# Tail values stored in tile order, block 14's own rows, one output round moved and the first feed-forward sums moved

## The chip, the cores and the metric

The program runs on one core of a Trainium2 chip. The core's engines run side by side, each with its own instruction queue: TensorE (PE; its weight loads are listed as PEld), VectorE (DVE), ScalarE (ACT), GpSimd (POOL) and SyncE (SP), which here only issues DMA transfers. They meet at semaphores: an instruction, or a separate semaphore instruction ahead of it, waits until a count is reached. The metric is the device time of one execution in microseconds, as the median of the runs. Smaller is better.

## The reference

The input x has 2048 rows of 640. A recurrent attention with 32 heads of 128 runs over 64 segments of 32 rows, carrying 8 memory rows from each segment to the next; a feed-forward part with a squared ReLU follows.

```python
for s in range(n_seg):                          # 64 segments
    xs = x[:, s * seg_len:(s + 1) * seg_len, :] # x is layernormed
    h = jnp.concatenate([mem, xs], axis=1)      # 8 + 32 rows
    q, k, v = (einsum('btd,dhe->bhte', h, W) for W in (Wq, Wk, Wv))
    scores = einsum('bhqe,bhke->bhqk', q, k) * scale
    scores = where(mask, scores, -1e9)          # memory columns open, the rest causal
    p = softmax(scores)
    o = einsum('bhte,hed->btd', einsum('bhqk,bhke->bhqe', p, v), Wo)
    mem = o[:, :M, :]                           # the next segment needs these rows
    outs.append(o[:, M:, :])
h  = x + concat(outs)
h2 = h + (relu(layernorm(h) @ w1 + b1) ** 2) @ w2 + b2
```

Only the 8 memory rows make the loop sequential. Segment s+1 can start once the memory rows of o are there; the other rows of a segment's output can be finished later.

## The kernel before

**Tiling.** A block is 128 rows, so four segments; there are 16 blocks (`NB`) and 64 steps (`NS`), one `step(b, sp)` for each segment. A step's projections take 32 rows: the 8 memory rows that the step before made and the first 24 rows of the segment (`HD`). The last 8 rows of a segment, its tail (`TL`), do not depend on the memory in q, k and v, so the tails of a block's four segments are projected together, 32 rows at a time, ahead of time. The weights wq, wk, wv and wo lie in SBUF, loaded once by SP at the start (`load_w`, `load_wo`).

**A step.** `step` writes the order of the work out by hand, and every engine executes it in that order: query and key projections (L234 in the helper `proj`), ScalarE's copies to `row` tiles and VectorE's 32 by 32 transposes to qT and kT; scores of the memory rows for each half of the heads (`scores`, L497); their softmax (`soft1`, `soft2`, `soft3`), which gives the transposed probabilities pB; value projections; token scores; the values of the memory rows for each half (`values`, L543 and L548, the second for the tail values `vt4`), copied to `oT` by ScalarE (`values_out`, L246); the output projection `wo_rounds` into the PSUM tile pw in 16 rounds of four matmuls (L270); `wo_out`, which adds the parts (L285 to L287) and transposes the new memory rows to `hT` (L382), with which the next step's query projection begins. Rounds 0 to 7 need the first half of the heads in `oT`, rounds 8 to 15 the second half. In a common step rounds 0 to 3 stand before `values` of the second half, and rounds 4 to 15 behind it. The token values of the segment before (`token_values`, L423 and L428) end the step on TensorE.

**Filler work.** TensorE is given independent work in between, from the list `fill`: the tail projections of coming blocks in units of five per half (`tail_units`), and the output projection of whole blocks' tails in ten units per block (`wo_tail_units`), which read the tail's attention output in `oTts` (two buffers for even and odd blocks). The plan has for each group of units a step by which it is due and a step from which it may be done. `portion(s)` takes units in the order of the due steps: as many as keep the running total at `round(8.15 * s)`, at most nine, and more where a due step has come. Other short work waits in lists too: `late` (at the start of a step, by a budget), `mid` (after the memory rows are made, two entries a step) and `nook` (one entry a step, between VectorE's token score subtraction, L657, and its sum, L664, while ScalarE computes the exponentials).

**Tail values.** `tail_out` writes the value rows of a block's tails from a `row` tile (or, at the start, from tiles that stand empty, `parked`) to the DRAM tile `vt_d`, and `tails_v_in` reads them back in the order that `values` needs, `vt4`. Before, `vt_d` has the layout of block, quarter of the columns (4), row (128), 256 columns. A write is one transfer of 128 rows by 2 pieces (L345); a read is four transfers of 32 partitions each (L402), one for each group of heads, and it fills vt4 a block ahead, in the second step of the block before. At the start the values of blocks 0 to 9 are projected; block 0's are written and read by POOL's queue (its last three quarters are read by SP), the others by SP, behind the load of wo.

**The end.** The step before last and the last fill in the first feed-forward tile's preparation: `prep_load`, `prep_sum0` (adding the attention output and x, L778), `prep_stats0`, `prep_norm0` and a transposing DMA, each for four blocks of rows in steps 57 to 63. In the last step SP loads w1 into the space of wq, after the query projections, and then the feed-forward part runs over four tiles of 512 rows (L994 and L1046).

Of the kernel before, what the change touches and what calls it, by code (L numbers as in the profile page):

```python
# [12 lines left out]
BF16 = mybir.dt.bfloat16  # L13
# [3 lines left out]
def kernel(  # L17
# [16 lines left out]
    nc = tc.nc  # L34
    _, S, D = A_x.shape
# [302 lines left out]
    def tail_out(b, which, n, ps, dve=False):  # L338
        row, wait = parked.pop(0) if which == "v" and 0 < b and parked else (rowtile()[:], False)
        evac_row(which, row, ps, dve)  # L340
        if which == "v":
            eng = nc.sync if b else nc.gpsimd

            def write():
                eng.dma_start(out=vt_d[b, 2 * n:2 * n + 2].rearrange("j r f -> r j f"),  # L345
                              in_=row.rearrange("r (j f) -> r j f", j=2))
            if wait:
                writes.append(write)
            else:
                write()  # L350
            return
        if n == 0:
            tails.setdefault(b, {})[which] = s2.tile([128, H, 32], BF16, tag=which + "Tt", name=which + "Tt")
        dst = tails[b][which]
        late.append((0.71, lambda: flip(row, dst, n), 4 * b - (which == "k")))

    def wo_tail_out(b, ps):
        o = wo_out(ps)
# [4 lines left out]
    def wo_tail_units(b):  # L363
        st = {}

        def out():
            wo_tail_out(b, st["ps"])

        def unit(k):
            def f():  # L370
                if k == 0:
                    st["ps"] = mmtile()
                wo_rounds(lambda p: oTts[b % 2][:, p, :], st["ps"], range(k * 16 // 10, (k + 1) * 16 // 10))
                return (False, out) if k == 9 else None
            return f
        return [unit(k) for k in range(10)]
# [13 lines left out]
        q = tails[b]["q"][:].rearrange("p h (k s) -> p h s k", s=4)[:, n * 16:(n + 1) * 16, sp, :]  # L390
        nc.gpsimd.tensor_copy(out=qT[:, n * 16:(n + 1) * 16, 0:TL], in_=q)

    vt4s = {}
    vt_d = dram.tile([NB, 4, 128, 2 * E], BF16)

    def tails_v_in(b, eng, s0=0, s1=4):

        if s0 == 0:
            vt4s[b] = s2.tile([128, 4, 2, E], BF16, tag="vt4", name="vt4")
        src = vt_d[b].rearrange("j (g k s) f -> g j k (s f)", g=G, s=4)  # L400
        for g in range(G):
            eng.dma_start(out=vt4s[b][32 * g:32 * g + 32, s0:s1].rearrange("p s u e -> p (s u e)"),  # L402
                          in_=src[g][:, :, s0 * 2 * E:s1 * 2 * E])

    def store_main(o, s):
        for q in range(4):
# [24 lines left out]
    def token_out(s, po):  # L431
        for h in range(2):
            gs = slice(2 * h, 2 * h + 2)
            nc.scalar.copy(out=oTg[:, gs, :, :, 0:SEG],  # L434
                           in_=po[1][h][:, :, 0:256].rearrange("p g (n j q) -> p g n j q", n=2, q=32))
        nc.gpsimd.tensor_copy(out=oTts[s // 4 % 2][:, :, s % 4 * TL:(s % 4 + 1) * TL], in_=oT[:, :, 0:TL])

    def spread(n):
        for a0, a1, f in ((0, 120, 3), (120, 128, 1)):
# [14 lines left out]
    def step(b, sp, v=None):  # L454
# [172 lines left out]
        skv = view()  # L627
        po = po_tiles()
        if last:
            run(fill, max(1, (len(fill) - 3) // 2), held, True)  # L630
            token_values(s - 1, *prevs[-2], po)
            token_out(s - 1, po)
            settle(held, True)
            run(fill, 2, held)
            settle(held, True)
            causal(skv)
        else:
            ahead = 0 if ready else (len(fill) + 1) // 2
            left = len(fill) - ahead
            run(fill, (ahead - 1) // 2, held, True)  # L640
            values(0, pT0, po[1][0])
            values_out(0, po[1][0])
            if not ready:
                nc.scalar.copy(out=v[:, 768:1024], in_=ps1[:, 256:512])
            run(fill, len(fill) - left, held)
            pw = chn.tile([128, 512], F32, tag="ch", name="pw")
            if not ready:
                wo_rounds(lambda p: oT[:, p, M:NK], pw, range(4))
            values(1, pT1, po[1][1])
            causal(skv)  # L650
            values_out(1, po[1][1])
            settle(held, True)
# [23 lines left out]
        if not last:  # L676
# [2 lines left out]
                    run(fill, SEG0[k])  # L679
                    wo_rounds(lambda p: oT[:, p, M:NK], pw, [2 * k + h for h in (0, 1, 8, 9)])  # L680
            else:
                wo_rounds(lambda p: oT[:, p, M:NK], pw, range(4, 16))
            o = wo_out(pw, ((s + 1) // 4, (s + 1) % 4), weigh)
            if s > 1:
                store_main(o, s - 2)
# [109 lines left out]
    def prep_sum0(k):  # L795
        pre[k] = prep_sum(0, k, pre[k])
# [100 lines left out]
            plan += [(4 * b - 3 + (which == "k"), 4 * b - 5, u[DC * n:DC * n + DC]) for n in range(2)]  # L897
    for b in range(10, NB):
        u = tail_units(b, "v")
        plan += [(b - 8 if b < 12 else 20 + 4 * (2 * b - 24 + n), 1 if b < 12 else 7, u[DC * n:DC * n + DC]) for n in range(2)]  # L900
    for b in range(NB - 1):
        plan.append((min(4 * b + 8, NS - 2), 4 * b + 5, wo_tail_units(b)))
    plan.sort(key=lambda p: p[0])
    begun, paced = [], [0]

    def portion(s):
        n = round(8.15 * s) - paced[0]
        got = []
        while True:
            if not begun:  # L910
# [14 lines left out]
    for b in range(NB):  # L925
        for sp in range(4):
# [25 lines left out]
            e = b * 4 + sp - (NS - 7)  # L952
            if (b, sp) == (1, 0):
                ffn_biases()
            if (b, sp) == (2, 0):
                nc.gpsimd.tensor_copy(out=b1f[:], in_=b1b[:])
            if 0 <= e < NK4:
                pre[e] = prep_load(0, e)
            if 1 <= e <= NK4:
                mid.append(lambda e=e: prep_sum0(e - 1))  # L960
            if 2 <= e <= NK4 + 1:
                late.insert(0, (1.15, lambda e=e: prep_stats0(e - 2), b * 4 + sp))
                mid.append(lambda e=e: prep_norm0(e - 2))
# [125 lines left out]
```

## Time and profile before

| what | value |
|---|---|
| median of 3 runs | 952.71 us (950.44 to 955.07) |
| profiled execution | 951.48 us, its span 949.7 us |
| granted TensorE clock, mean | 0.996 |
| busy share: PE, DVE, ACT, POOL | 97%, 72%, 60%, 33% |
| first query matmul of step 1 | 62.89 us |
| first query matmul of step 63 | 807.61 us |
| first feed-forward matmul | 818.33 us |
| SP's transfers: o_all stores, vt reads, vt writes | 320, 64, 30 |

The span goes from the first to the last instruction of the program; the profiled execution's time has some 1.8 us around it. The start up to 62 us is the loading of the weights; then come 62 steps of about 12 us; from 818 us on the feed-forward. An engine's busy share is an average over these stages. A matmul's record lasts longer than the distance between matmuls' starts, since they are pipelined and four run beside each other on 32 columns of the array each, so distances between starts are what counts for TensorE. In the timeline a row merges equal instructions that follow each other: start, time, engine, line, operation, operands, count, and in brackets the engine's idle time before it with what ended it.

### The profile page before, as it was taken

The page shows a single profiled execution, that of the slowest core. Times are in us where ns is not written, and L with a number is a line of the kernel's source. Part 1 is how long each engine was busy: PE and PEld are TensorE (multiplying, and loading weights), DVE is VectorE, ACT ScalarE, POOL GpSimd, SP SyncE. Part 2 cuts the span into 40 slices and gives each one's busy share as a digit, 9 for nine tenths or more (in the row PEclk, how much of TensorE's full clock was granted, in tenths as well). Part 3 has the DMA queues.
Part 4 walks back from the last instruction along what each step waited for, and adds up shares of the span by engine and source line. Part 5 has one row for each costly group of instructions (what it writes and reads, how often), then busy time and mean ns, then how long its engine had stood idle before and what let it go on. Part 6 is the DMA issues. An engine that isn't in the chain of part 4 may idle for free.

```text
span 949.7 us, 56126 instructions
## 1 busy us (share of the span) xinstructions
PE 923.1 (97%) x24760; PEld 530.0 (56%) x24760; DVE 681.8 (72%) x2068; ACT 570.9 (60%) x1586; POOL 311.7 (33%) x1002
## 2 busy tenths in 40 slices
PE   5979999999999999999999999999999999999998
PEld 2435555555565555555555555556555655565555
DVE  5167788777877777777778777877777788556632
ACT  2546667666766666666667666766676666523321
POOL 2113333333333333333333333333333334344300
PEclk9989999999999999999999999999999999999999
DMA  9982200010001000010101010101010112723320
GB/s 349 405 269 65 42 23 23 20 27 17 20 22 25 20 20 25 17 29 9 32 14 31 14 33 13 33 13 31 9 33 8 52 44 20 239 75 91 91 56 28
DMA packets 65876, 56.67 MB, mean 60 GB/s; under 512 B 37384, under 2 KB 61712, under 8 KB 63712
## 3 DMA queue, kind: packets, MB, share of 16 engines
q1 hardware_dynamic: 65392, 52.74, 19.4%
q8 instruction: 194, 3.18, 1.4%
q14 instruction: 50, 0.41, 0.1%
q0 software_dynamic: 224, 0.33, 0.1%
q10 hardware_dynamic: 16, 0.01, 0.0%
HBM read 38.37 MB, written 9.44 MB: 50 GB/s over the span
## 4 chain that ended last, share of the span: by engine, by line
PE 88%; DMA 5%; DVE 3%; SPq 2%; ACT 1%; issue 1%; POOL 0%; DVEq 0%; ACTq 0%
PE ps L234 22%; PE px L234 21%; PE pw L270 15%; PE pk L234 7%; PE y L1046 6%; PE ps L994 6%; PE ps L270 3%; DMA wq<-in_A_Wq_dram 2%; PE po L543 2%; PE po L423 2%; SPq L151 2%; PE sm L497 1%; PE ps L593 1%; PE po L548 1%; DMA wo<-in_A_Wo_dram 1%
## 5 line engine op out<-in xcount | busy, mean ns | idle before, releaser
L234 PEld LDWEIGHTS <-hT 128*32 128x32 bf16 x7680 | 181.7, 96 | 162.1 <-DVE hT L382 22.6
L270 PE MATMUL pw<-wo,oT 128*32 128x320 bf16 x4224 | 169.4, 299 | 3.4 <-DMA wo<-in_A_Wo_dram 2.3
L234 PE MATMUL px<-wv,hT 128*32 128x512 bf16 x2520 | 166.3, 377 | 0.0
L270 PEld LDWEIGHTS <-oT 128*32 128x32 bf16 x4224 | 108.2, 96 | 43.5 <-ACT oT L246 20.0
L258 DVE STREAM_TRANSPOSE qT<-row 128x512 bf16<-128x512 bf16 x128 | 89.0, 696 | 32.3 <-ACT row L253 32.1
L671 POOL TENSOR_TENSOR pkt<-ek,rk 128x64 bf16<-128x64 bf16 x64 | 19.0, 296 | 261.8 <-ACT otmp L286 255.6
L234 PE MATMUL ps<-wq,hT 128*32 128x512 bf16 x1260 | 82.7, 385 | 3.8 <-DVE hT L382 2.8
L234 PE MATMUL ps<-wk,hT 128*32 128x512 bf16 x1280 | 80.4, 379 | 0.0
L234 PE MATMUL px<-wq,hT 128*32 128x512 bf16 x1260 | 79.4, 379 | 0.0
L234 PE MATMUL pk<-wk,hT 128*32 128x512 bf16 x1240 | 79.2, 383 | 0.0
L1002 ACT ACTIVATE wv<-ps,b1f 128x512 bf16<-128x512 f32 (+1 forms) x56 | 37.6, 672 | 66.8 <-PE ps L994 66.0
L434 ACT CAST oT<-po 128x512 bf16<-128x512 f32 x128 | 68.7, 589 | 10.3 <-PE po L428 5.5
L234 PEld LDWEIGHTS <-hTt 128*32 128x32 bf16 x1920 | 51.5, 97 | 36.8 <-issue 3.5
L246 ACT CAST oT<-po 128x128 bf16<-128x128 f32 x126 | 33.5, 267 | 63.8 <-PE po L548 61.1
L443 POOL COPY qz<-qT 128x96 bf16<-128x96 bf16 x126 | 33.6, 267 | 111.0 <-DVE qT L258 110.6
L1046 PE MATMUL y<-wq,wk 128*128 128x320 bf16 x416 | 58.9, 299 | 0.2
L484 ACT CAST row<-ps 128x256 bf16<-128x256 f32 x126 | 40.8, 375 | 29.9 <-PE ps L234 29.1
L253 ACT ACTIVATE row<-ps 128x512 bf16<-128x512 f32 x93 | 54.8, 611 | 5.4 <-PE ps L234 4.3
L285 ACT COPY otmp<-pw 64x96 f32<-64x96 f32 (+2 forms) x129 | 28.9, 224 | 48.0 <-PE pw L270 27.5
L253 ACT ACTIVATE row<-px 128x512 bf16<-128x512 f32 x63 | 37.6, 597 | 32.1 <-PE px L234 32.1
L287 DVE TENSOR_TENSOR o<-pw,otmp 128x96 bf16<-128x96 f32 (+2 forms) x129 | 31.4, 243 | 30.0 <-ACT otmp L286 23.9
L497 PEld LDWEIGHTS <-qz 128*32 128x32 bf16 x2016 | 35.7, 95 | 27.9 <-POOL qz L443 2.1
(138 smaller groups left out, 1858.3 us busy)
## 6 DMA issues: line engine op xcount, KB each, us to landing
wv<-in_A_Wv_dram SPq DMA_DIRECT2D x5, 1024.0 KB
wq<-in_A_Wq_dram SPq DMA_DIRECT2D x5, 1024.0 KB
wk<-in_A_Wk_dram SPq DMA_DIRECT2D x5, 1024.0 KB
wo<-in_A_Wo_dram SPq DMA_DIRECT2D x8, 640.0 KB
o_all<-o SPq DMA_DIRECT2D x256, 7.5 KB
vt<-vt_d SPq DMA_DIRECT2D x60, 64.0 KB
xt<-in_A_x_dram SPq DMA_DIRECT2D x19, 160.0 KB
wq<-in_B_w_dram SPq DMA_DIRECT2D x1, 2080.0 KB
```

What stands on the lines that cost most here:

```text
L234: nc.tensor.matmul(ps[32 * k:32 * k + 32, :], lhsT=lhs(c), rhs=wr[:, c, n, k], start=(c == 0), stop=(c == DC - 1))
L246: nc.scalar.copy(out=out_, in_=in_)
L253: nc.scalar.mul(out=row, in_=ps, mul=scale)
L258: nc.vector.transpose(out=dst[:, n * 16:(n + 1) * 16, 0:32], in_=row.rearrange("p (h e) -> p h e", e=32))
L270: nc.tensor.matmul(pw[32 * j:32 * j + 32, c0:c0 + DH], lhsT=lhs(p), rhs=wov2[:, head(p), ch], start=(h == 0), stop=(h == 15))
L434: nc.scalar.copy(out=oTg[:, gs, :, :, 0:SEG], in_=po[1][h][:, :, 0:256].rearrange("p g (n j q) -> p g n j q", n=2, q=32))
L443: nc.gpsimd.tensor_copy(out=d.rearrange("p a (j f) -> p a j f", j=3)[:, :, :, 0:M], in_=src[:, :, 0:3, :])
L484: nc.scalar.copy(out=row[:, u * 256:(u + 1) * 256], in_=ps[:, u * 256:(u + 1) * 256])
L497: nc.tensor.matmul(sm[32 * g:32 * g + 32, 0:NK], lhsT=qz[:, p, :], rhs=kT[:, p, :], start=(j == 0), stop=(j == 3), skip_group_check=True)
L994: nc.tensor.matmul(ps[:], lhsT=w1[:, c, fc * 128:(fc + 1) * 128], rhs=hnT[:, c, :], start=(c == 0), stop=(c == DC - 1))
L1002: nc.scalar.activation(out=r[:, 0:w], in_=ps[:, 0:w], func=ACT.Relu, bias=b1f[:, fc:fc + 1], scale=1.0)
L1046: nc.tensor.matmul(y[hh][:, 0:DH], lhsT=f1T[:, fc, k * 128:(k + 1) * 128], rhs=w2[:, fc, cs], start=(fc == 0 and not hf), stop=(fc == FFUL ...
```

## The change

It has four parts. The tail values' DRAM tile `vt_d` gets the order of group of heads, quarter, row, and 256 columns, so that a block is read by one transfer of 128 partitions instead of four of 32, and a write becomes two transfers of half the columns each, whose DRAM side has the four groups as its first dimension. Block 14's tail output gets rows of its own: two tiles with the tag of `hTt` in place of half of `oTts` (`late_tails`, `tail_part`), filled by two POOL copies. With this the due steps move: block 14's tail output projection is due in step 63 in place of 62, block 12's in 61 in place of 56, the late value units eight steps later, and the pace becomes 8.05 units a step, with fixed totals in steps 61 and 62; the last step runs its filler as two units before the token values and the rest behind them. The fifth output round (four matmuls) goes from behind the second `values` to before it. And `prep_sum0` goes from `mid` to `nook`.

```diff
             def write():
-                eng.dma_start(out=vt_d[b, 2 * n:2 * n + 2].rearrange("j r f -> r j f"),
-                              in_=row.rearrange("r (j f) -> r j f", j=2))
+                for j in range(2):
+                    eng.dma_start(out=vt_d[b, :, 2 * n + j].rearrange("g k s f -> g (k s) f"),
+                                  in_=row[:, j * 2 * E:(j + 1) * 2 * E])
...
+    def tail_part(b, h):
+        if b in late_tails:
+            return late_tails[b][h]
+        return oTts[b % 2][:, h * 16:(h + 1) * 16, :]
...
-                wo_rounds(lambda p: oTts[b % 2][:, p, :], st["ps"], range(k * 16 // 10, (k + 1) * 16 // 10))
+                wo_rounds(lambda p: tail_part(b, p // 16)[:, p % 16, :], st["ps"], range(k * 16 // 10, (k + 1) * 16 // 10))
...
-    vt_d = dram.tile([NB, 4, 128, 2 * E], BF16)
+    vt_d = dram.tile([NB, G, 4, TL, 4, 2 * E], BF16)
...
-        src = vt_d[b].rearrange("j (g k s) f -> g j k (s f)", g=G, s=4)
-        for g in range(G):
-            eng.dma_start(out=vt4s[b][32 * g:32 * g + 32, s0:s1].rearrange("p s u e -> p (s u e)"),
-                          in_=src[g][:, :, s0 * 2 * E:s1 * 2 * E])
+        eng.dma_start(out=vt4s[b][:, s0:s1].rearrange("p s u e -> p (s u e)"),
+                      in_=vt_d[b].rearrange("g j k s f -> (g j k) (s f)")[:, s0 * 2 * E:s1 * 2 * E])
...
-        nc.gpsimd.tensor_copy(out=oTts[s // 4 % 2][:, :, s % 4 * TL:(s % 4 + 1) * TL], in_=oT[:, :, 0:TL])
+        if s // 4 not in late_tails:
+            nc.gpsimd.tensor_copy(out=oTts[s // 4 % 2][:, :, s % 4 * TL:(s % 4 + 1) * TL], in_=oT[:, :, 0:TL])
+            return
+        for h in range(2):
+            nc.gpsimd.tensor_copy(out=tail_part(s // 4, h)[:, :, s % 4 * TL:(s % 4 + 1) * TL],
+                                  in_=oT[:, h * 16:(h + 1) * 16, 0:TL])
...
         if last:
-            run(fill, max(1, (len(fill) - 3) // 2), held, True)
+            run(fill, 2, held, True)
             token_values(s - 1, *prevs[-2], po)
             token_out(s - 1, po)
             settle(held, True)
-            run(fill, 2, held)
+            run(fill, 100, held)
...
-                wo_rounds(lambda p: oT[:, p, M:NK], pw, range(4))
+                wo_rounds(lambda p: oT[:, p, M:NK], pw, range(5))
...
-                wo_rounds(lambda p: oT[:, p, M:NK], pw, range(4, 16))
+                wo_rounds(lambda p: oT[:, p, M:NK], pw, range(5, 16))
...
-        plan += [(b - 8 if b < 12 else 20 + 4 * (2 * b - 24 + n), 1 if b < 12 else 7, u[DC * n:DC * n + DC]) for n in range(2)]
+        plan += [(b - 8 if b < 12 else 28 + 4 * (2 * b - 24 + n), 1 if b < 12 else 7, u[DC * n:DC * n + DC]) for n in range(2)]
     for b in range(NB - 1):
-        plan.append((min(4 * b + 8, NS - 2), 4 * b + 5, wo_tail_units(b)))
+        plan.append(({NB - 4: NS - 3, NB - 2: NS - 1}.get(b, min(4 * b + 8, NS - 3)), 4 * b + 5, wo_tail_units(b)))
...
-        n = round(8.15 * s) - paced[0]
+        n = {NS - 3: 482, NS - 2: 486}.get(s, round(8.05 * s)) - paced[0]
...
+            if (b, sp) == (NB - 2, 0):
+                two = [s2.tile([128, DC, 4, TL, 4], BF16, tag="hTt", name="oTl", bufs=4) for _ in range(2)]
+                late_tails[b] = [x[:].rearrange("p c b k s -> p (c b k s)")[:, 0:512].rearrange("p (h r) -> p h r", r=32)
+                                 for x in two]
...
             if 1 <= e <= NK4:
-                mid.append(lambda e=e: prep_sum0(e - 1))
+                nook.append(lambda e=e: prep_sum0(e - 1))
```

More of the change, by code (lines that the diff above doesn't have):

```diff
@@ L391, in tails_q_in @@
         nc.gpsimd.tensor_copy(out=qT[:, n * 16:(n + 1) * 16, 0:TL], in_=q)
-    vt4s = {}
-    vt_d = dram.tile([NB, 4, 128, 2 * E], BF16)
+    vt4s, late_tails = {}, {}
+    vt_d = dram.tile([NB, G, 4, TL, 4, 2 * E], BF16)
     def tails_v_in(b, eng, s0=0, s1=4):
```

## The prediction

> **What bounds the kernel now.** I read the page first, then the timeline of single steps, then the DMA share in short windows.
>
> ```profile
> span 949.7 us, 56126 instructions
> PE 88%; DMA 5%; DVE 3%; SPq 2%; ACT 1%; issue 1%; POOL 0%; DVEq 0%; ACTq 0%
> ```
>
> The first line is the span, the second the chain that ended last. TensorE carries 88% of it. A step is measured in the timeline from the first query matmul to the next step's. Steps 22 and 23 (315.63 to 327.41 to 339.18) take 11.77 us each, the commonest value; steps 2 to 62 average 11.99. So the excess over 11.77 is 13 us in all, and what the change can win inside the steps is part of that. The stretch that the fifth output round touches, in the timeline of step 23:
>
> ```profile
> 335.41 0.73 PE L270 MATMUL pw<-wo,oT 128*32 128x320 bf16 x16
> 335.43 0.45 DVE L525 STREAM_TRANSPOSE pB<-pm 128x256 bf16<-128x256 bf16 x1
> ...
> 336.01 0.28 PE L543 MATMUL po<-pB,v 128*32 128x32 bf16 x16
> 336.12 0.24 PE L548 MATMUL po<-pB,vt 128*32 128x128 bf16 x4
> ...
> 336.17 1.82 PE L270 MATMUL pw<-wo,oT 128*32 128x320 bf16 x48
> ...
> 336.40 0.27 ACT L246 CAST oT<-po 128x128 bf16<-128x128 f32 x1 [0.84 <-PE po L548]
> ...
> 336.72 0.94 PEld L270 LDWEIGHTS <-oT 128*32 128x32 bf16 x32 [0.16 <-ACT oT L246]
> ```
>
> Four rounds (16 matmuls) run from 335.41. The second values group waits for VectorE's pB (L525 ends 335.88) and starts at 336.01. Then four more rounds hide ScalarE's copy of its result (336.40 to 336.67); the rounds that need that copy load weights at 336.72. The first values group of a block's first step (step 8):
>
> ```profile
> 154.89 0.28 PE L543 MATMUL po<-pB,v 128*32 128x32 bf16 x16
> 155.17 0.24 PE L548 MATMUL po<-pB,vt 128*32 128x128 bf16 x4
> ```
>
> L548 follows L543 after 0.28 us, against 0.11 in step 23. The view of line L548 shows why: TensorE's queue executes separate semaphore waits there, 33 in the run, for the four transfers that brought the tail values.
>
> ```profile
> L548 PEldq EVENT_SEMAPHORE  x33: 51/51/51, 54.5 to 779.0; - x33
> ```
>
> Windows (the last two columns are DMA share and GB/s). The first holds a read of tail values, whose DRAM side begins with a dimension of four; the second holds writes, whose sides begin with 128 rows:
>
> ```profile
> 742.20:745.60 3.40, 3.40 (x128) 2.46 (x124) 2.66 (x8) 2.08 (x6) 0.00 (x0) 1.00 0.25 78
> 93.00:94.00 1.00, 1.00 (x52) 0.55 (x38) 0.99 (x4) 0.94 (x4) 0.52 (x3) 1.00 0.92 260
> ```
>
> A transfer beginning with four runs at a quarter of the DMA capacity.
>
> **The change part by part.**
>
> *Fifth round before the wait (L647 to L657 of the kernel after).* A round is 48 matmuls' stretch over 12: with start-to-start spacing 1.63/12 it costs 0.135 us. In step 23 the next free slot after round 4 is 0.135 x 4 after 335.41, 335.95, so TensorE really waits only 0.06 us for pB. A fifth round puts the values group 0.07 late. Behind it, three rounds are left to cover the way values, ScalarE, weights (336.14 last start to 336.72, 0.58 us), where four fit exactly. So the late rounds start 0.07 later, and so does all after them: the round fills 0.06 and opens 0.13. Step 37 has an extra 0.217 us filler unit ahead of the same place and lasts 11.87: delay there is paid. The cost is 0.07 in about 48 steps with pB in time, none in the eight or so where VectorE is late (steps 13, 18, 21, 26, 43, 51): +3.4 us. Ends: -3.7 (61 x 0.06, if the later wait were covered) and +8.2 (61 x 0.135).
>
> *One read a block.* The four-semaphore wait becomes one. Steps 8, 12, 16, 28, 36 last 11.87 to 11.91; 14 such steps less 0.12: -1.7 (ends 0 and 15 x 0.18 = -2.7). SP issues 15 x 3 fewer reads at 609 ns.
>
> *Two writes for one.* The write's DRAM side now begins with the four groups. The near row is the read at share 0.25: 260 GB/s at share 0.92 makes 71 GB/s on a quarter, 0.92 us for 64 KB, so 1.84 a unit against 0.50 now. Who waits: at the start SP writes seven parked units behind the wo load, whose data fill the DMA until about 60.8, and the read of block 0's other tails is queued behind them:
>
> ```profile
> 52.65 2.56 SPq L345 DMA_DIRECT2D vt_d<-parkv  x2
> ...
> 61.03 2.77 SPq L402 DMA_DIRECT2D vt<-vt_d  x4
> ...
> 72.11 0.24 PE L548 MATMUL po<-pB,vt 128*32 128x128 bf16 x4
> ```
>
> The share is 1.08 from 52.7 to 60.8, so they get through from 59.5 to 60.8 on; 14 x 0.92 ends at 72.4 to 73.7, and with the read (0.7) and a landing (0.3, an estimate) that is 73.4 to 74.7 against 72.1: +1.7 in step 1 (ends 0 and 4). Later parked writes (SP has 42 in place of 21 up to step 3) queue, but their readers are 20 us off. A row buffer is rewritten only when both its writes have landed; by the program's waits only the unit finished at the end of step 11 is close: issued about 2.3 us into step 12 behind the o_all stores, landed at 5.4 (0.6 for the first issue, 1.84 of data, 0.7 estimated for start and landing, which no view shows for SP), wanted by ScalarE's L493 at 4.6: +1.1 (ends 0 and 1.5), on the chain, since the exponentials queue behind it on ScalarE. POOL's two write issues become four (0.86 each) at 22 us, where POOL then idles 13.8 us: nothing; its four reads become one. SP issues of the four-group shape cost 0.59 (L361) for 0.40: SP is idle then.
>
> The Trainium skill, page "DMA: Bandwidth & Descriptors", section "Why a DMA increments its semaphore by 16 and not by 1", states that the number of DMA engines is the largest up to 16 dividing the slowest dimension of both sides. By that rule these writes get four engines; the windows agree (0.25 against 0.92), and the rule speaks against this part of the change by the same 1.7 + 1.1 us.
>
> *Pacing and deadlines.* From the instruction order, the before kernel gives nine filler units (0.217 us each) or more in steps 4, 10, 17, 24, 31, 37, 44, 50, 57 and nearly none in 60 and 62; after gives eight nearly everywhere. Excess of those steps over their neighbours: 0.1 to 0.2 each, 0.4 and 0.5 in steps 10 and 50, 1.9 together; three nine-unit steps return 0.6: -1.3 (ends 0 and -3). Empty steps 60 and 62 lasted 12.16 and 12.04, so emptiness won nothing there.
>
> *First sums in VectorE's wait.*
>
> ```profile
> 757.68 0.49 DVE L664 TENSOR_REDUCE zk<-ek 128x8 f32<-128x320 bf16 x1 [0.59 <-ACT ek L662]
> ...
> 759.57 0.86 DVE L778 TENSOR_TENSOR ht<-ot,ht 128x640 bf16<-128x640 bf16 x1
> ...
> 763.74 0.28 PE L497 MATMUL sm<-kT,qz 128*32 128x40 bf16 x16 [0.19 <-DVE kT L258]
> ```
>
> The sum (0.86) stands ahead of the next step's transposes, and the scores of steps 59 to 62 start 0.36, 0.43, 0.27 and 0.31 late: -1.4. Moved into the 0.59 wait it overruns by 0.27 and makes L287 some 0.1 late, four times: +0.4. Net -1.0 (ends +0.4, if those scores stay late, and -2). The Trainium skill, "GPSIMD Engine Reference", section on its specifications, says that GpSimd shares SBUF interfaces with VectorE where VectorE reads two SBUF inputs. By it the sum takes 0.48 in the new place, where POOL is idle, as L778's other twelve do (median 484 ns), and the +0.4 vanishes; no run before shows that place.
>
> *Block 14's own rows.* POOL copies two halves instead of one, four times some 0.2 us more; POOL is 33% busy and kT's tails (L387) are wanted 3 us later: nothing (end +0.8). Its output moves to steps 61 to 63. In step 63, 12 of 28 matmuls fit the wait before 817.65, 16 follow (0.54):
>
> ```profile
> 811.79 1.09 SPq L727 DMA_DIRECT2D wq<-in_B_w_dram  x2
> ...
> 817.65 0.37 PE L423 MATMUL po<-pTk,v 32*128 32x32 bf16 x30 [0.62 <-ACT v L616]
> ...
> 818.33 2.33 PE L994 MATMUL ps<-hnT,wq 128*128 128x512 bf16 x10 [0.23 <-DMA wq<-in_B_w_dram]
> ```
>
> SP loses four stores (2.54 us at 806.10) ahead of the weight load, which then issues some 0.7 earlier; the feed-forward is no longer held by it but by TensorE, 818.1 + 0.54 = 818.65: +0.3 (ends -0.7 and +1).
>
> Sum: 3.4 - 1.7 + 1.7 + 1.1 - 1.3 - 1.0 + 0.3 = +2.5 us. The profiled execution took 951.48 (span 949.7), so 954.0 against itself. Its time lies 1.2 below the median of the runs, 952.71; the mean of the four executions is 952.4, 0.9 above the profiled one, and I add that: 954.9.
>
> **The rivals.** *A, slower: the write transfers on a quarter of the DMA.* If the backlog also catches block 1's transposed rows (42 x 0.92 + 2.5 from 60 ends at 101.1, landed 102.4, wanted at 100.2 by step 4), and the ends hold in step 1 (4.0) and step 12 (1.5), it costs 7.7 where I counted 2.8: 959.8. It decides where the landing of block 0's read passes 74.5. For it: share 0.25. Against it: readers far away, and each stall lets the backlog drain. *B, faster: the fifth round fills the wait for nothing.* If ScalarE's copy were not what releases the late rounds, 48 steps win 0.06 instead of losing 0.07: 954.9 - 6.3 = 948.6. For it: the wait for pB is there. Against it: the 0.16 idle behind ScalarE's L246 is already there with four rounds. *C: the rearrangement does not do what it says:* the sums stay costly (+0.4 for -1.0) and block-first steps keep their length because pB bounds them (0 for -1.7): 958.0. Against it: step 8's L548 gap stands on TensorE itself.
>
> **How the numbers follow.** The forecast has 0.56, A 0.21, B 0.13, C 0.10. The range reaches B's time at the low end and A's at the high end: 948.8 to 960.0; it leaves out about 0.2. A change of 0.5%, 4.8 us, is about what a measurement tells from none (the runs spread from 950.44 to 955.07): 947.95 and 957.47 are the bounds. Slower: nearly all of A, half of C, 0.05 of the forecast, 0.30. Faster: half of B and 0.05 of the forecast, 0.12. Same: 0.58.
>
> **What would show it.** L543's second start against L525's end and the idle before the weights behind L246: about 0.3 instead of 0.16 if I am right on the fifth round; step length about 11.84. L548 0.11 behind L543 in steps 8, 12, 16. DMA share 0.25 while vt_d is written, and a wait at L548 in step 1. Scores without delay in steps 59 to 62. The prediction is wrong if common steps last 11.77 or less, or if the wait in step 1 is above 3 us.

## The result and the profile after

The change makes the kernel slower. The median of six runs is 963.69 us (960.58 to 965.37) against 951.47 us (950.43 to 955.07) for six runs of the kernel before; the ratio is 1.0119, with an interval of 1.0095 to 1.0143, or 9 to 14 us. The forecast was 954.9 us in a range of 948.8 to 960.0, so the time lies above the range. The profiled execution took 960.58 us (span 958.8), the fastest of the six; against its counterpart before (span 949.7) it is 9.1 us longer, and those 9.1 us can be placed.

The page's span and its chain by engine, kernel after:

```profile
span 958.8 us, 56073 instructions
PE 92%; DVE 3%; issue 2%; DMA 2%; ACT 1%; POOL 0%; SPq 0%; DVEq 0%; ACTq 0%; POOLq 0%
```

The chain looks better than before: TensorE has 92% of it instead of 88%, DMA 2% instead of 5%. Shares of a whole span do not show the loss; a table by stage does. The boundaries are the first query matmuls of the steps in the timeline:

| stage | before, us | after, us | difference |
|---|---|---|---|
| start, up to step 1 | 62.89 | 73.06 | +10.17 |
| step 1 | 13.64 | 12.03 | -1.61 |
| steps 2 to 62 | 731.08 | 731.65 | +0.57 |
| step 63 and feed-forward | 142.09 | 142.06 | -0.03 |
| span | 949.7 | 958.8 | +9.1 |

The whole loss is in the start, a stage in which the prediction counted the change at nothing. The timeline of the start, POOL, ScalarE and TensorE (start, duration, engine, line, operation, and in brackets the idle time before it and what ended it):

```profile
21.32 0.94 POOL L346 DMA_DIRECT2D vt_d<-row  x1 [0.61 <-ACT row L246]
28.02 0.71 POOL L346 DMA_DIRECT2D vt_d<-row  x1 [5.76 <-issue]
36.68 0.69 POOL L346 DMA_DIRECT2D vt_d<-row  x1 [7.95 <-issue]
43.27 0.69 POOL L346 DMA_DIRECT2D vt_d<-row  x1 [5.89 <-issue]
...
49.84 0.60 POOL L406 DMA_DIRECT2D vt<-vt_d  x1 [5.06 <-DMA vt_d<-row]
49.33 0.60 ACT L253 ACTIVATE row<-pa 128x512 bf16<-128x512 f32 x1 [12.25 <-DMA vt_d<-row]
49.98 1.04 PE L234 MATMUL pa<-wk,hTt 128*32 128x512 bf16 x8 [11.70 <-ACT row L253]
```

Read it from the bottom. TensorE stood 11.70 us for ScalarE's L253, which copies a row of the query projection out of PSUM. L253 stood 12.25 us because its row buffer was still being read by a write of block 0's tail values (vt_d<-row). And that write was late because POOL issued it late: its four writes went out at 21.32, 28.02, 36.68 and 43.27, with "issue" in front of three of them, which is time in which the engine waited for nothing that the profile shows. POOL's program has no semaphore wait ahead of the second write either. Nor does VectorE hold POOL: it did nothing from 25.35 to 31.72 and from 37.89 to 49.96, and two of the late issues lie in these stretches. The semaphores that tell when a transfer's data have arrived, its landing, give the pattern: the four writes landed at 27.70, 36.38, 42.96 and 49.23, so each issue follows the landing of the one before by 0.3 us. Before, the two writes stood back to back:

```profile
22.08 1.73 POOL L345 DMA_DIRECT2D vt_d<-row  x2 [1.31 <-ACT row L246]
```

The kernel has four row buffers, and these two units of values hold two of them. The third row of the query projection reuses the first unit's buffer just as that becomes free (36.38), the fourth reuses the second unit's and waits for 49.23. Before, both units had landed by 30.8.

Step 1 gives 1.61 us back: with the start late, the output weights had all landed when they were wanted, and the low clock that in the kernel before stretched step 1 fell into the start (last section).

The steps themselves came out nearly as forecast. The stretch around the fifth round, timeline of step 23 (the stretch shown of before, now with 20 matmuls ahead; L543 and L548 of before are L552 and L557 here):

```profile
344.83 0.45 DVE L534 STREAM_TRANSPOSE pB<-pm 128x256 bf16<-128x256 bf16 x1
344.93 0.86 PE L270 MATMUL pw<-wo,oT 128*32 128x320 bf16 x20
345.61 0.28 PE L552 MATMUL po<-pB,v 128*32 128x32 bf16 x16
...
345.72 0.24 PE L557 MATMUL po<-pB,vt 128*32 128x128 bf16 x4
...
345.77 1.83 PE L270 MATMUL pw<-wo,oT 128*32 128x320 bf16 x44
346.01 0.27 ACT L246 CAST oT<-po 128x128 bf16<-128x128 f32 x1 [1.06 <-PE po L557]
346.33 0.94 PEld L270 LDWEIGHTS <-oT 128*32 128x32 bf16 x32 [0.30 <-ACT oT L246]
```

The idle ahead of the late weights is 0.30 us, where it was 0.16, and the commonest step takes 11.86 us instead of 11.77. And in a block's first step L557 now follows L552 after 0.10 us instead of 0.28, since it waits for one transfer (step 8, timeline of TensorE):

```profile
164.04 0.27 PE L552 MATMUL po<-pB,v 128*32 128x32 bf16 x16
164.14 0.24 PE L557 MATMUL po<-pB,vt 128*32 128x128 bf16 x4
```

### The profile page after: what moved, and what is told of

Same layout as the page of the kernel before. It is cut to its first block, busy times and chain, and to the rows that moved or that the text cites. A ratio compares the mean times of both kernels' runs of the same rounds, so it can differ in the third digit from the quotient of the medians.

```text
span 958.8 us, 56073 instructions
## 1 busy us (share of the span) xinstructions
PE 923.2 (96%) x24749; PEld 528.5 (55%) x24760; DVE 681.9 (71%) x2068; ACT 571.0 (60%) x1586; POOL 311.6 (32%) x1005
## 4 chain that ended last, share of the span: by engine, by line
PE 92%; DVE 3%; issue 2%; DMA 2%; ACT 1%; POOL 0%; SPq 0%; DVEq 0%; ACTq 0%; POOLq 0%
PE ps L234 24%; PE px L234 21%; PE pw L270 16%; PE pk L234 7%; PE y L1059 6%; PE ps L1007 6%; PE ps L270 3%; PE po L427 2%; PE po L552 2%; PE sm L506 1%; PE ps L602 1%; DMA wv<-in_A_Wv_dram 1%; PE po L557 1%; PE pa L234 1%; DMA vt_d<-row 1%
## 5 line engine op out<-in xcount | busy, mean ns | idle before, releaser
L270 PE MATMUL pw<-wo,oT 128*32 128x320 bf16 x4224 | 176.4, 300 | 0.5 <-ACT oT L246 0.2
L253 ACT ACTIVATE row<-ps 128x512 bf16<-128x512 f32 x93 | 54.9, 611 | 5.4 <-PE ps L234 4.0
L253 ACT ACTIVATE row<-px 128x512 bf16<-128x512 f32 x63 | 37.6, 597 | 32.1 <-PE px L234 32.1
L287 DVE TENSOR_TENSOR o<-pw,otmp 128x96 bf16<-128x96 f32 (+2 forms) x129 | 31.4, 244 | 28.7 <-ACT otmp L286 21.1
L496 DVE STREAM_TRANSPOSE kT<-row 128x256 bf16<-128x256 bf16 x126 | 48.6, 424 | 2.7 <-ACT row L493 0.2
```

What stands on the lines that cost most here:

```text
L253: nc.scalar.mul(out=row, in_=ps, mul=scale)
L270: nc.tensor.matmul(pw[32 * j:32 * j + 32, c0:c0 + DH], lhsT=lhs(p), rhs=wov2[:, head(p), ch], start=(h == 0), stop=(h == 15))
L496: nc.vector.transpose(out=dst[:, n * 16 + u * 8:n * 16 + u * 8 + 8, 0:32], in_=row[:, u * 256:(u + 1) * 256].rearrange("p (h e) -> p h e", ...
```

## The experiments

Twelve kernels ran. Ratios are to the kernel before on the same chip; differences in us are a kernel's median less that kernel's. "Step 1 starts" and step lengths are from each run's own timeline.

**Spreading POOL's four writes.** What if block 0's values leave POOL in transfers that all DMA engines share?

```diff
             def write():
+                if b == 0:
+                    for g in range(G):
+                        eng.dma_start(out=vt_d[b, g, 2 * n:2 * n + 2].rearrange("j k s f -> (k s) j f"),
+                                      in_=row[32 * g:32 * g + 32, :].rearrange("r (j f) -> r j f", j=2))
+                    return
                 for j in range(2):
```

> The changed kernel, but block 0's tail values are written from POOL in four transfers a unit, one for each group of heads (32 rows by two quarters), so that each is spread over all DMA engines; SP's writes stay as in the change. Theory 1 (in the changed kernel POOL could not issue a four-group write before the one ahead of it had landed, so the four issues stood at 21.3, 28.0, 36.7 and 43.3 us, and ScalarE's fourth query row waited 12.25 us for a row buffer): POOL issues all eight within about 7 us, step 1 starts at 63 to 64 us instead of 73.1, step 1 itself is long again (13.6 and up to 1.7 more, since the output weights land only at 61), and the time is 963.7 - 10.2 + 1.6 to 3.3, that is 955.1 to 956.8. Rival (the four-group writes are slow wherever they are issued, SP's eighteen at the start included): step 1 starts or ends late all the same, time above 959.

Measured: 955.23 us (ratio 1.0046, 1.0032 to 1.0060; +4.6). The timeline of POOL and VectorE:

```profile
21.68 4.47 POOL L347 DMA_DIRECT2D vt_d<-row  x8 [1.09 <-ACT row L246]
...
77.37 0.49 DVE L186 BATCH_NORM_STATS2 lnsx<-xt 128x6 f32<-128x320 bf16 x1 [3.45 <-DMA xt<-in_A_x_dram]
78.45 0.28 DVE L393 STREAM_TRANSPOSE hT<-o 128x96 bf16<-128x96 bf16 x1
```

All eight issues stand in one block of 4.47 us, and step 1 starts at 62.38. So the wait ahead of POOL's issues comes from the shape of its writes, and it was worth the 10.2 us of the start. The time lies inside the 955.1 to 956.8 expected, but in part by luck, since the rest is not what was expected: not a late read of block 0's tails (L562 follows L557 after 0.11 us), but VectorE's statistics L186, which waited until 77.4 for rows of x. They stand ahead of the hT transposes (L393), so the queries of step 2 start 2.66 us late; step 1 lasts 16.40 and step 2, at a low clock, 13.54.

**Own tiles for block 0's values.** By which way does the late landing reach the path?

```diff
+        if which == "v" and b == 0:
+            row, wait = oT[:].rearrange("p h k -> p (h k)")[:, n * 512:n * 512 + 512], False
+        else:
+            row, wait = parked.pop(0) if which == "v" and parked else (rowtile()[:], False)
-        row, wait = parked.pop(0) if which == "v" and 0 < b and parked else (rowtile()[:], False)
```

> The changed kernel, but block 0's two units of tail values go through oT, which is free until step 1, instead of two of the four row buffers. Theory 1 with the row buffers as the only way the late landing reaches the path: POOL's issues still stand at 21, 28, 36 and 43, but ScalarE's L253 does not wait, step 1 starts at 63 to 65, time 955 to 958. Rival (the path runs through POOL itself, whose qz copies and read of the tail values stand behind those issues): step 1 starts at 69 or later, time above 960.

Measured: 955.36 us (1.0054, 1.0034 to 1.0074). POOL's issues stand one behind another as in the changed kernel, at 21.80, 30.43, 38.55 and 45.79, but step 1 starts at 64.18 (timeline, the last issue and the first query matmul):

```profile
45.79 0.69 POOL L349 DMA_DIRECT2D vt_d<-oT  x1 [6.55 <-issue]
...
64.18 1.30 PE L234 MATMUL ps<-wq,hT 128*32 128x512 bf16 x20 [1.19 <-DVE hT L391]
```

So nearly all of the delay went through the row buffers. About 1.8 us against the run above (64.18 to 62.38) is left to POOL itself: its copies of the key tails behind the read, which could be issued only at 52.6, held the first scores 3.35 us, and TensorE's clock was 0.60 from 58 to 64; the wait for the output weights covers part of it.

**The new DRAM order alone.** The kernel before, with only the lines of `vt_d` (shape, write, read) from the diff.

> The kernel before with only the new order of the tail values in DRAM (two four-group writes a unit, one read a block). Theory 1: POOL's write issues stand one behind another as in the changed kernel, step 1 starts 10 us late; 1.6 of it comes back in step 1, since the output weights have landed by then, and the block-first steps lose their extra 0.12 (14 times): 951.5 + 10.2 - 1.6 - 1.7 = 958.4. Rival (the late start comes from another part of the change, such as the order of the work): step 1 starts at 63 and the time is 950 to 953.

Measured: 961.92 us (1.0114, 1.0091 to 1.0137; +11.3). POOL issues at 20.91, 27.76, 36.70 and 43.54, step 1 starts at 73.16 and lasts 12.25. This part alone loses as much as the whole change; the time is 3.5 us above the number expected, and the profiled steps 2 to 62 (732.1 us) do not show in sum the 1.7 us that the single read should give back, though the block-first steps 12, 28 and 36 do take 11.75 to 11.78.

**What makes POOL wait.** The same four-group shape for block 0's values, with half the rows in each transfer:

```diff
+                    for j in range(2):
+                        for h in range(2):
+                            eng.dma_start(out=vt_d[b, :, 2 * n + j, 4 * h:4 * h + 4].rearrange("g k s f -> g (k s) f"),
+                                          in_=row[64 * h:64 * h + 64, j * 2 * E:(j + 1) * 2 * E])
```

> A measurement of the disputed wait: the changed kernel, but block 0's tail values go out from POOL in eight four-group transfers of 16 rows a group for four of 32 (half the 512-byte rows each; the rows land in another order, so the tail values of block 0 are not the reference's). If the wait comes from how many rows of a transfer each DMA engine holds at a time (32 of two transfers at once went through before, 32 + 32 did not), the first two issues go back to back, and from then on an issue follows about every landing: the eight end at about 40 to 45 us as the four did. If any transfer on four DMA engines makes the next wait, seven waits of 6 us stand one behind another and the last issue comes after 60 us. If the number of bytes decides, more than two go back to back, since two of 128 KB did before.

Measured, one run: 955.88 us; step 1 starts at 63.70. The timeline of POOL:

```profile
20.80 2.11 POOL L348 DMA_DIRECT2D vt_d<-row  x3 [0.90 <-ACT row L246]
26.71 0.63 POOL L348 DMA_DIRECT2D vt_d<-row  x1 [3.79 <-issue]
27.74 0.62 POOL L348 DMA_DIRECT2D vt_d<-row  x1 [0.40 <-issue]
29.96 0.62 POOL L348 DMA_DIRECT2D vt_d<-row  x1 [1.60 <-issue]
33.06 1.39 POOL L348 DMA_DIRECT2D vt_d<-row  x2 [2.48 <-issue]
```

Three go out at once, not two and not all. They landed at 26.40, 27.43 and 29.65, and the fourth, fifth and sixth issue follow at 26.71, 27.74 and 29.96: each issue comes 0.31 us behind the landing of the one three places ahead. So it is not that a transfer on four DMA engines makes the next one wait, and not bytes: three of 32 KB filled what two of 128 KB did not. Counted in rows of 512 bytes for each DMA engine that carries data, three times 16 fit and a fourth 16 did not; in the change 32 fit and a second 32 did not; before, two times 16 fit. All three agree with room for at least 48 and fewer than 64 such rows in flight on POOL's queue; the queue itself stands in no view. That four DMA engines carry the data is read from the packet records: a POOL write of the change has 16 packets of 4,096 bytes and 48 of 32 bytes, one of half the size 8 and 24, and the spread ones have none of 32; twelve times a quarter of the large ones looks like filling for twelve engines without data, which is an inference. The issues ended at 34.5 us and not at 40 to 45 as expected, since the landings overlapped.

**Four rounds in the changed kernel.**

```diff
-                wo_rounds(lambda p: oT[:, p, M:NK], pw, range(5))
+                wo_rounds(lambda p: oT[:, p, M:NK], pw, range(4))
...
-                wo_rounds(lambda p: oT[:, p, M:NK], pw, range(5, 16))
+                wo_rounds(lambda p: oT[:, p, M:NK], pw, range(4, 16))
```

> The changed kernel with the fifth output round back behind the second values group. Theory (the fifth round opens the cover of ScalarE's copy, 0.26 idle ahead of the late weights against 0.13): common steps take 11.77 again instead of 11.86, 0.09 in some 48 steps: 963.7 - 4.3 = 959.4. Rival (the round fills TensorE's wait for pB and costs nothing): 963.7 within 1.5. The start is untouched by both: step 1 at 73.

Measured: 960.33 us (1.0102, 1.0074 to 1.0130), between the two expectations. The common step is 11.77 again; the start is 1.6 us longer in this execution (74.66), as POOL's waits depend on when a landing comes.

**The fifth round alone**, on the kernel before (the two lines the other way round).

> The kernel before with the fifth output round alone put ahead of the second values group. Theory (the late weights then wait for ScalarE's copy): the commonest step goes from 11.77 to 11.86 and the time rises by 0.09 in 48 to 61 steps, 4.3 to 5.5 us. Rival (the round fills a wait): no rise, or up to 3.7 us less.

Measured: 954.42 us (1.0035, 1.0019 to 1.0051; 3.3 us by the ratio, 1.8 to 4.8). The commonest step goes from 11.77 to 11.86. The theory holds; the sum is a little under it.

**Pacing and block 14's rows alone.** The kernel before with `late_tails`, the due steps, 8.05 units a step and the last step's split:

```diff
-        plan += [(b - 8 if b < 12 else 20 + 4 * (2 * b - 24 + n), 1 if b < 12 else 7, u[DC * n:DC * n + DC]) for n in range(2)]
+        plan += [(b - 8 if b < 12 else 28 + 4 * (2 * b - 24 + n), 1 if b < 12 else 7, u[DC * n:DC * n + DC]) for n in range(2)]
...
-        n = round(8.15 * s) - paced[0]
+        n = {NS - 3: 482, NS - 2: 486}.get(s, round(8.05 * s)) - paced[0]
```

> The kernel before with only block 14's own tail rows, the later due steps, the pace of 8.05 units and the last step's filler split (old DRAM order, four rounds, first sums where they were). Theory by the prediction's rows: nine-unit steps become eight-unit ones, -1.3 us (0 to -3), the end +0.3. Rival (the work is only moved, TensorE executes the same units): within 0.5 us of before. The trace should show steps 4, 10, 17, 24, 31, 37, 44, 50, 57 at 11.77 to 11.9 under the first, and the sum of steps 2 to 62 down by 1.3.

Measured: 950.46 us (0.9997, 0.9983 to 1.0011; one of the twelve executions took 2369.05 us and is not in the ratio). In the profile, steps 2 to 62 sum to 728.2 us against 731.1, seven of the nine steps named are 0.1 to 0.7 us shorter and two are longer (17 and 31), and the end is 1.0 longer (143.1 to 142.1). The time is not told apart from before. Both theories remain possible. Why the end is longer stays open: it is long in the next run too (143.6), but not in the kernel after (142.1), whose last step has the same filler.

**Pacing and the first sums.** As above, and `nook.append(lambda e=e: prep_sum0(e - 1))` for `mid.append(...)`.

> The kernel of the pacing run, and the first feed-forward sums in VectorE's wait as well: all parts of the change but the DRAM order and the fifth round. Theory: the scores of steps 59 to 62 start without delay, 1.0 to 1.4 us less than the pacing run alone, so 2 to 2.5 us under before. Rival (the sums only delay another consumer): the same time as the pacing run.

Measured: 949.48 us (0.9977, 0.9960 to 0.9995), faster than before and 1.0 us under the run without the sums, though those two intervals overlap. The sum takes 0.48 us in its new place, where it took 0.86 (VectorE's timeline, first the pacing run, then this one):

```profile
767.63 0.86 DVE L788 TENSOR_TENSOR ht<-ot,ht 128x640 bf16<-128x640 bf16 x1
```

```profile
767.15 0.48 DVE L788 TENSOR_TENSOR ht<-ot,ht 128x640 bf16<-128x640 bf16 x1
```

Step 59 goes from 12.20 to 11.86, step 61 from 12.32 to 11.78 and step 62 from 12.55 to 12.17; step 60 stays (11.77 and 11.79).

**Every write over all DMA engines.** The changed kernel with four rounds, and the loop over groups of heads (first experiment) for all blocks, so SP issues four writes a unit.

> The changed kernel with four output rounds, and with every write of tail values as four transfers of 32 rows (one for each group of heads, both quarters), which all DMA engines share; one read a block stays. Theory (the write's shape on four DMA engines was the loss, and the single read is worth what the prediction gave it): no POOL issue waits, step 1 starts at 62 to 63 and lasts 13.6 to 14, block-first steps lose 0.12, time 2 to 2.5 us under before by pacing and sums and 1.7 more by the read: 946.5 to 948.5 on a chip where before takes 950.6. Rival (SP's queue, with four issues a unit for one, now delays block 1's rows): steps 1 and 2 above 14 and 12.5, time 949.5 or more.

Measured: 966.52 us (1.0168, 1.0150 to 1.0187): the rival, and far beyond it. Step 1 starts at 62.73 but lasts 23.33 us, and steps 2, 3 and 4 take 14.20, 17.31 and 13.69. SP's timeline, and the waits for transfers between 62 and 125 us (total, times, longest):

```profile
52.47 8.65 SPq L346 DMA_DIRECT2D vt_d<-parkv  x8
61.21 4.73 SPq L346 DMA_DIRECT2D vt_d<-oTt  x8
66.04 3.66 SPq L346 DMA_DIRECT2D vt_d<-spare  x8
69.80 2.72 SPq L346 DMA_DIRECT2D vt_d<-parkx  x4
72.84 0.34 SPq L406 DMA_DIRECT2D vt<-vt_d  x1
73.24 0.42 SPq L122 DMA_DIRECT2D xt<-in_A_x_dram  x1
73.70 8.49 SPq L346 DMA_DIRECT2D vt_d<-hnT  x16
82.30 0.36 SPq L122 DMA_DIRECT2D xt<-in_A_x_dram  x1
```

```profile
DVE lnsx L186 <- DMA xt<-in_A_x_dram: 10.3, 1, 10.3
DVE lnst L158 <- DMA xt<-in_A_x_dram: 7.3, 1, 7.3
PE ps L234 <- DMA hT<-xn: 5.5, 1, 5.5
PEld L557 <- DMA vt<-vt_d: 3.3, 1, 3.3
```

The DMA engines are not full (share 0.29 to 0.40 from 62.7 to 86 us); late is what SP issues behind the writes. The read of block 0's tails stands behind 28 of them (TensorE waits 3.2 us, the wait that the prediction put into step 1, by another way), block 2's rows behind 44 (10.3 us on VectorE, 6.4 on TensorE). Later it is the transposing load of block 1's rows, issued at 114.75 (5.5 us on TensorE), and the tail rows of x behind it (7.3 on VectorE). From step 5 on this kernel is cheap: steps 5 to 62 sum to 690.4 us against 692.9 in the pacing and sums run, which reads a block by four transfers, and the block-first steps 8, 12, 16, 28 and 36 take 11.74 to 11.82 us against 11.87 to 11.95. That is the single read's gain, 0.13 to 0.17 us a block.

**The load of block 1's rows first.** The first experiment's kernel, with `load_x(1)` directly behind `load_wo()`.

> The run with POOL's writes spread over all DMA engines, and in addition SP issues the load of block 1's rows ahead of the tail-value writes and not behind eighteen of them. Theory (after the start is mended, what is left is block 1's rows: VectorE's statistics L186 waited for them until 77.4 in step 1, and the idle brought a clock of 0.62 in step 2): step 1 goes from 16.4 to 13.6 to 14 and step 2 from 13.5 to 12.0, 4 us less: 951 on a chip where before takes 950.6. Rival (the writes hold the DMA engines themselves, so that the rows land late wherever they are issued, or block 0's read and the next loads are late instead): above 953.5.

Measured: 956.54 us (1.0058, 1.0036 to 1.0080): the theory fell. Step 1 lasts 17.02 and L186 still waits for rows whose load SP issues at 73.39, behind eight writes. In the chain that load follows SP's L351; by the order of SP's instructions it is the second one, block 2's, behind the parked units that SP writes in step 1.

**The same with four rounds.**

> The same with four output rounds ahead of the second values group for five. Theory: 4 to 5 us less than with five rounds, and by the single read 1.7 less than the run with pacing and sums alone: 946.5 to 948, under the kernel before by 3 to 4. Rival (the single read gives nothing here): as the run with pacing and sums, 949.5.

Measured: 951.06 us (0.9999, 0.9987 to 1.0011). Against the run above that is 5.5 us for the fifth round; the expected 946.5 to 948 fails by the load of block 2's rows, which is late here too (step 1 16.55, step 2 14.42).

**The load of block 2's rows first.** Spread POOL writes and four rounds; `load_x(1)` where it was, and in step 1 the parked writes behind `load_x(2)`:

```diff
-            if b == 0 and sp:
+            if b == 0 and sp > 1:
                 run(writes, 4)
...
             if b + 2 < NB and sp == 1:
                 load_x(b + 2)
                 nook += ln_parts(b + 2)
+            if b == 0 and sp == 1:
+                run(writes, 4)
```

> POOL's writes spread over all DMA engines and four output rounds, as in the last run but one part: block 1's rows are loaded where they were, and in step 1 SP issues the load of block 2's rows ahead of the four parked units and not behind them. The runs before showed that it is this second load (issued at 73.4 us behind eight four-group writes, landed at 77.4) that VectorE's statistics wait for in step 1, and that the first load's place makes no difference. Theory: step 1 goes from 16.5 to 13.6 to 14 and step 2 from 14.4 (a clock of 0.6 after the idle) to 12, 4.5 us less than the 951.1 of the run with four rounds: 946.5. Rival (the data of the writes hold the DMA engines, so that the load lands late from its new place too): above 949.5.

Measured: 945.46 us against 948.25 for before on this chip (0.9973, 0.9960 to 0.9985; -2.8). The timeline, and the page's span:

```profile
66.74 0.90 SPq L122 DMA_DIRECT2D xt<-in_A_x_dram  x2
67.68 5.64 SPq L351 DMA_DIRECT2D vt_d<-hnT  x8
...
73.58 0.48 DVE L186 BATCH_NORM_STATS2 lnsx<-xt 128x6 f32<-128x320 bf16 x1
```

```profile
span 943.4 us, 56084 instructions
```

L186 no longer waits; step 1 takes 13.42 and step 2 12.20, where they took 16.55 and 14.42. Queue order on SP, not the DMA engines, was the second loss. This kernel is faster than the one before, by 0.27%; the run with pacing and sums alone is too, by 0.23%, and the intervals overlap, so the new DRAM order, once mended, gains nothing that a time can show over the old one.

## Why the prediction was wrong

**The step that failed** is one sentence under "Two writes for one": "POOL's two write issues become four (0.86 each) at 22 us, where POOL then idles 13.8 us: nothing". An issue was priced by its duration on the engine, and the idle time behind it was taken for cover. The runs show that the second issue waits for the landing of the first, 6 to 8 us while the weights load, that this happens three times, and that the units sit in row buffers that ScalarE needs: +10.2 us in the start, 1.6 of it returned in step 1. Spreading the writes gave the start back (62.38), and the row buffers alone gave nearly all of it (64.18). The prediction did ask what a four-group write costs by its data (0.92 us) and to issue (0.86 on POOL, 0.59 on SP); what POOL's issue can wait for was not asked. The question that it put to the later units, when both writes of a row buffer land, it did not put to these two.

**Writes on a quarter of the DMA.** Tail-value writes alone on the DMA, in the windows of the kernel after (the last three columns are the granted clock, DMA share and GB/s):

```profile
88.00:89.00 1.00, 1.00 (x24) 0.48 (x20) 1.00 (x3) 0.51 (x2) 0.81 (x3) 1.00 0.27 74
```

0.27 and 74 GB/s, as forecast (a quarter, 71). The Trainium skill, "DMA: Bandwidth & Descriptors", section "Why a DMA increments its semaphore by 16 and not by 1", gives these writes four engines; the trace agrees (0.27 of the capacity). But the two prices that hung on it are not there: in the kernel after, the late start leaves time for the read in step 1 (+1.7 forecast, no wait), and step 12 takes 11.91 (+1.1 forecast). With the start mended (first experiment) the read of block 0's tails is still in time, and step 12 takes 11.90, so both prices were wrong and not only covered. No run shows the 0.3 and 0.7 us that they took for a landing; the one landing of SP's that a reader waited for in the first experiment came 4.0 us after its issue (block 2's rows). The 1.1 is also 0.8 by its own times (5.4 against 4.6). What the shape costs on SP is another thing. The prediction priced these issues at 0.59 us and at nothing, since "SP is idle then"; in the first experiment they took 0.7 to 1.5 us, and the load of block 2's rows stood behind them: 4.4 us in steps 1 and 2 (16.40 + 13.54 against 13.64 + 11.92). The prediction asked who reads what SP writes, and not who waits for what SP loads behind those writes.

**Rival A** had the right cause (the write's shape) and direction, at a chance of 0.21, but another place and another mechanism: a backlog of data in step 1, block 1's rows and step 12. With the start mended (first experiment) the time is 4.6 us above before, nearly all of it (4.4 in steps 1 and 2) from SP's order of issues. That its 959.8 us lies nearest to the 963.69 measured is luck. **Rivals B and C** are excluded: the fifth round costs time, and the block-first steps do lose their 0.12.

**The fifth round.** +3.4 forecast; 3.3 (1.8 to 4.8) measured alone, 5.5 between the two runs with block 1's rows first, and 1.7 in steps 2 to 62 between the profiles of the changed kernel with five rounds and with four; and the way it was argued: 0.30 us idle ahead of the weights, 11.86 us a step (11.84 forecast). **One read a block.** 0.13 to 0.17 a block-first step, where 0.12 was forecast; no single run's time resolves it. **Pacing and block 14's rows.** -1.3 + 0.3 forecast, -0.3 (-1.6 to +1.0) measured. **The sums.** -1.0 forecast; the two runs differ by 1.0, inside the uncertainty. The sum takes 0.48 in the wait, which the prediction had from the Trainium skill, "GPSIMD Engine Reference", its section on specifications; the trace agrees: POOL stands idle beside it there, and in the old place POOL's L683 runs beside it. The +0.4 that its -1.0 holds for a late L287 is not seen: in the step shown, L287 starts at 768.15, right behind ScalarE's copy (768.12). Without the start and step 1, the forecast's terms make 3.4 - 1.7 + 1.1 - 1.3 - 1.0 + 0.3 = +0.8 us, and the two profiles differ by 0.57 - 0.03 = +0.5. That this fits is partly luck, as the +1.1 in it was not there.

**What stays open.** The medians differ by 12.2 us and the profiled executions by 9.1; the profiled one is the fastest of its six. The start differs by up to 1.6 us between the profiled runs of this shape (73.06, 73.16, 74.66), but the other executions have no trace.

## What to carry to other kernels

Ask of a transfer not only how long it runs but what its issue can wait for and which buffer it holds until it lands: here an issue of 0.7 us became a wait of 6 to 8 us three times over, at a place where the engine stood idle. When a write changes shape, count its rows for each DMA engine, and look on its queue for the small load that somebody waits for: one such load, not the amount of data, made up the second loss in the first experiment, and with every write spread four transfers came late in this way. And a saving on the queue of one engine can be taken back on another: the single read won 0.13 us and more a block, and the writes that made it possible cost 10 us in the start.

## What the runs showed of the hardware

- POOL's write issues waited, without any semaphore, for the landing of transfers ahead of them: with 48 rows of 512 bytes in flight for each DMA engine that carries data they went through, with 64 they did not, as at a full queue. The issue then followed a landing by 0.3 us.
- SP's issues of four-group writes took 1.5 us each at 52 us and 0.7 at 67.5 in the first experiment (four in 5.84 us, eight in 5.72), and writes spread over all DMA engines still 0.5 to 1.1 us each where SP issued 28 of them in a row.
- Idle time of TensorE had a second price here: after the longer waits the granted clock was low for some 4 to 5 us. After 1.38 us of waiting, at 73.06 in the kernel after, it stayed at 1.00. In the first experiment, windows around the late start of step 2 (TensorE busy, its clock, DMA share, GB/s):

```profile
76.00:78.80 2.80, 0.14 (x18) 1.00 0.16 57
78.80:80.30 1.50, 1.50 (x24) 0.81 0.06 11
80.30:84.00 3.70, 3.70 (x48) 0.62 0.18 51
84.00:92.00 8.00, 8.00 (x270) 1.00 0.23 68
```

The 2.66 us of waiting made step 1 longer, and 3.7 us at 0.62 made step 2 13.54 us long. In the kernel before the same low clock (0.61 from 64.2 to 67.6) follows the waits for the output weights (0.96 and 1.33 us) and for hT (1.17) and stretches step 1 to 13.64; in the kernel after it fell at 50 to 54 us (0.52), behind the wait of 11.70 us, inside the start.
